# Down projection, attention output and denominators moved onto two 64-row tiles of the array

## The chip, the cores and the metric

The kernel runs on one core of a Trainium2 chip. The metric is device time in microseconds (us) of one execution. Its profile is one execution taken by the hardware profiler.

## What is computed

One block of a transformer on 2048 tokens of width 576: a layer norm, then linear attention with 32 heads of 18 and a gated feed-forward layer (FFN) of width 4608, both on the normed input, both added to the input. Cut to what matters:

```python
xn = layernorm(x)
q, k, v = split_heads(xn @ wqkv)                  # 32 heads of 18
phi = lambda t: where(t > 0, t + 1, exp(t)) + 1e-6
pq, pk = phi(q), phi(k)
kv = einsum("bhsd,bhse->bhde", pk, v)
z = einsum("bhsd->bhd", pk)
o = einsum("bhqd,bhde->bhqe", pq, kv) / (einsum("bhqd,bhd->bhq", pq, z)[..., None] + 1e-6)
out = x + o @ wo + (gelu(xn @ w_gate) * (xn @ w_up)) @ w_down
```

## The kernel before, in words

The order of instructions on each engine is the order of the program; a framework adds the semaphores. Work goes in three parts.

**Attention, to about 65.7 us.** Steps listed with due times (`STEPS`, lines 486 to 503, sorted at 535) norm the 16 tiles of 128 tokens, transpose them, compute the keys' phi and the sums over tokens. Queries are kept transposed in `pqT`: five chunks of heads (7, 7, 7, 7 and 4 heads: four times 126 rows, then 72) by 2048 tokens. `zrep` and `kvT` hold, per chunk, the sums of keys repeated per head and the key-value products, masked to the heads' diagonal blocks.

**FFN, gate and up** (`gu_pair`, line 615). The tokens go in four groups of 512 (`sc`), the 4608 hidden columns in blocks of 256. The contraction over 576 is four and a half tiles of 128 rows, so it is done on two tiles of the array of 64 rows each: a `_Unit` (line 302) has two outputs in two PSUM banks. In its first turn (`p1`) the lower rows feed output 0 while the upper rows feed output 1; in its second turn (`p2`) they change over. The units are built so that the two row tiles take turns on a bank; between the turns stands a relay: an empty instruction on another engine waits for the last matmul of the first turn, and the second turn waits for it (lines 322 and 323, 328 and 329). For gate and up the relay is on SyncE in the very first block and on GpSimd in all later ones (line 630). Between the two turns of a unit stands the other unit's first turn. ScalarE applies GELU (line 647), VectorE multiplies by the up half and writes `hT` (line 648). The eight PSUM banks go round in a ring, `banks`.

**FFN, down** (`down_tile`, line 664). For each of the four groups, the four tiles of 128 tokens are done in two halves of 288 output columns: 36 matmuls over `hT` and `wd_sb` (line 677), then five more that add the attention's output (line 682): `pqT`, by then divided by the denominators, times `m_sb`. Each is a full matmul of 128 rows (126 or 72 for the attention). VectorE adds the input and writes the result (line 685), SyncE stores it.

Two things lie inside the down stages. In the first one, `m_stage` (line 654) computes `m_sb`, the product of `kvT` and the output weights, chunk by chunk before steps 0, 6, 12, 18 and 24 of the first half, copied out by ScalarE (line 662). In the first three, the denominators of the next 512 tokens are made: one chunk per half tile, starting with the second, before its step 0 (`dn`, line 704): a matmul of `zrep` by `pqT` (`den_mm`, line 448), an evacuation by VectorE (line 445), four reciprocals by VectorE and the scaling of `pqT` by GpSimd (`den_norm`, lines 469 to 478). The denominators of tokens 0 to 511, and of the fifth chunk of tokens 512 to 1023, were made during the first gate and up blocks as units on two row tiles (`den_pair`, line 454).

**Start.** The x tiles 4 to 15 and the query weights are loaded by SyncE after VectorE has written two elements of x tile 4 (the step at time 4.0, lines 532 to 534), so that step sets when those loads begin.

Of the kernel before, what the change touches and what calls it, by code (L numbers as in the profile page):

```python
# [9 lines left out]
ALU = mybir.AluOpType  # L10
BF16 = mybir.dt.bfloat16
# [16 lines left out]
HALF = D // 2  # L28
KT = 5
HCH = [7, 7, 7, 7, 4]  # L30
HOFF = [0, 7, 14, 21, 28]
NCH = len(HCH)
CR = 7 * DH
# [23 lines left out]
def kernel(  # L57
# [11 lines left out]
    nc = tc.nc  # L69
# [12 lines left out]
    fwork = ctx.enter_context(tc.tile_pool(name="fwork", bufs=3))  # L82
# [9 lines left out]
    def load_x(n0, cnt):  # L92
        nc.sync.dma_start(x_sb[:, n0:n0 + cnt, :], x_view[:, n0:n0 + cnt, :])
# [47 lines left out]
    zrep = persist.tile([P, NCH, CR], BF16, name="zrep")  # L141
    kvT = persist.tile([P, NCH, CR], BF16, name="kvT")

    nc.vector.memset(pqT[HP:P, NCH - 1, 0:2 * SC], 0.0)
    nc.vector.memset(zrep[HP:P, NCH - 1, :], 0.0)

    def load_wo():
        nc.sync.dma_start(wo2[:CR, 0:4, :], A_wo[0:4 * CR, :].rearrange("(c p) j -> p c j", p=CR))
# [153 lines left out]
    class _Unit:  # L302
# [12 lines left out]
                start=start, stop=stop, skip_group_check=True,  # L315
            )

        def p1(self):
            for kt in self.first:
                self.mm(0, LO, kt, kt == self.first[0], False)  # L320
                last = self.mm(1, HI, kt, kt == self.first[0], False)
            self.turn = self.relay.nop()
            tc.add_manual_dep(self.turn.ins, last.ins.name, SYNC, reason="the row tiles take turns on a bank")

        def p2(self):
            for kt in self.then:
                m = self.mm(1, LO, kt, False, kt == self.then[-1])
# [114 lines left out]
    def den_evac(sc, c, ps):  # L442
        rows = DH * HCH[c]
        d = dwork.tile([P, SC], F32, name="den_sb", tag="den_sb", bufs=6)
        nc.vector.tensor_scalar_add(out=d[:rows, :], in0=ps, scalar1=EPS_ATT)
        den_sb[sc, c] = d

    def den_mm(sc, c, bank):
        rows = DH * HCH[c]
        ps = ps_all[:rows, bank, :]  # L450
        nc.tensor.matmul(ps, lhsT=zrep[:rows, c, :rows], rhs=pqT[:rows, c, sc * SC:(sc + 1) * SC], start=True, stop=True)  # L451
        den_evac(sc, c, ps)

    def den_pair(items, outs):

        rows = DH * HCH[items[0][1]]

        def part(r):

            return slice(r.start, min(r.stop, P if rows <= P - HP + 8 else rows))  # L460

        return _Unit(
            outs,
            lambda i, r, kt: zrep[part(r), items[i][1], :rows],
            lambda i, r, kt: pqT[part(r), items[i][1], items[i][0] * SC:(items[i][0] + 1) * SC],
            nc.sync, first=(0,), then=(0,),
        )

    def den_norm(sc, c, q, pieces):
        w = SC // pieces  # L470
        rows = DH * HCH[c]
        d = den_sb[sc, c][:rows, q * w:(q + 1) * w]
        cols = slice(sc * SC + q * w, sc * SC + (q + 1) * w)
        for h in range(0, w, P):
            nc.vector.reciprocal(out=d[:, h:h + P], in_=d[:, h:h + P])  # L475

        def scale():
            nc.gpsimd.tensor_tensor(out=pqT[:rows, c, cols], in0=pqT[:rows, c, cols], in1=d, op=ALU.mult)  # L478
        return scale
# [135 lines left out]
    def gu_pair(sc, k):  # L615
        cs = slice(sc * SC, (sc + 1) * SC)
        blk = sc * (NF // GUB) + k
        wg, wu, wr = gu_blocks.pop(blk)
        units = []
        for i in range(GUB):  # L620
            b = [banks.next(), banks.next()]
            fcol = slice(i * P, (i + 1) * P)

            def lhs(a, rows, kt, fcol=fcol):
                if kt == 4:
                    return wr[rows, fcol]
# [12 lines left out]
        den = None  # L639
        if sc == 0 and 0 <= k - DEN_FROM < len(DEN_PAIRS):  # L640
            items = DEN_PAIRS[k - DEN_FROM]
            den = den_pair(items, [ps_all[:DH * HCH[c], banks.next(), :] for _, c in items])
            den.p1()
        for i, (b, u) in enumerate(units):
            u.p2()
            gl = fwork.tile([P, SC], F32, name="gl")
            nc.scalar.activation(out=gl[:], in_=ps_all[:, b[0], :], func=ACT.Gelu_apprx_tanh)  # L647
            nc.vector.tensor_tensor(out=hT[:, GUB * k + i, :], in0=ps_all[:, b[1], :], in1=gl[:], op=ALU.mult)  # L648
# [5 lines left out]
    def m_stage(c, acc_bank):  # L654
        rows = DH * HCH[c]
        for hf in range(2):
            b = (acc_bank + 2 + (2 * c + hf) % 6) % 8
            hs = slice(hf * HALF, (hf + 1) * HALF)
            nc.tensor.matmul(  # L659
                ps_all[:rows, b, :HALF], lhsT=kvT[:rows, c, :rows], rhs=wo2[:rows, c, hs], start=True, stop=True,  # L660
            )
            nc.scalar.copy(out=m_sb[:rows, c, hs], in_=ps_all[:rows, b, :HALF])

    def down_tile(sc, j, hooks):
        n = sc * TPC + j
        ts_ = slice(n * P, (n + 1) * P)
        res = fwork.tile([P, D], BF16, name="res")
        last = n == NS - 1
        for hf in range(2):
            hs = slice(hf * HALF, (hf + 1) * HALF)  # L670
            todo = hooks.pop(0) if hooks else {}
            acc_bank = banks.next()
            acc = ps_all[:, acc_bank, :HALF]
            for f in range(NF):
                if f in todo:
                    todo[f](acc_bank)
                nc.tensor.matmul(  # L677
                    acc, lhsT=hT[:, f, j * P:(j + 1) * P], rhs=wd_sb[:, f, hs], start=(f == 0), stop=False,
                )
            for c in range(NCH):  # L680
                rows = DH * HCH[c]
                nc.tensor.matmul(  # L682
                    acc, lhsT=pqT[:rows, c, ts_], rhs=m_sb[:rows, c, hs], start=False, stop=(c == NCH - 1),
                )
            nc.vector.tensor_tensor(out=res[:, hs], in0=acc, in1=x_sb[:, n, hs], op=ALU.add)  # L685
            if last:
                nc.sync.dma_start(out_view[:, n, hs], res[:, hs])
        if not last:
            nc.sync.dma_start(out_view[:, n, :], res[:])

    for sc in range(NSC):
        for k in range(NF // GUB):
            gu_pair(sc, k)
            if scales:
                scales.pop(0)()
            if den_jobs and k > DEN_FROM:
                scales.append(den_norm(*den_jobs.pop(0)))
        while wd_loaded[0] < NF:
            load_wd_slice()

        hooks = [{6 * c_: (lambda b, c_=c_: m_stage(c_, b)) for c_ in range(NCH)} if sc == 0 else {}]
        if sc + 1 < NSC:
            for c_ in range(NCH):
                def dn(b, c=c_, nsc=sc + 1):
                    if (nsc, c) not in den_sb:
                        den_mm(nsc, c, (b + 2) % 8)
                    den_norm(nsc, c, 0, 1)()
                hooks.append({0: dn})
        for j in range(TPC):
            down_tile(sc, j, hooks)  # L710


# [28 lines left out]
```

## Time and profile before

| what | us |
|---|---|
| median of 3 runs (523.57 to 524.0) | 523.75 |
| the profiled execution | 523.47 |
| its span, first to last instruction | 521.7 |
| attention, 0 to 65.7 | 65.7 |
| gate and up, four groups | 77.2, 70.05, 70.0, 70.05 |
| down, four groups, the last one with the end of the kernel | 42.5, 41.45, 41.4, 43.35 |

How to read the lines that follow in the prediction: a row of forty digits is the span cut in forty slices, each digit the busy share in tenths; PEclk is the clock granted to TensorE. "L313 PE MATMUL ps_all<-xnT,wg 64\*128 64x512 bf16 x1152 | 272.6, 376 | 0.0" is a group: line, engine, operation, output and inputs, rows by columns of weights, shape, count, then busy time in us and mean ns of one, then the engine's idle time ahead of them. Matmuls are pipelined, so the length of one (286 ns for 288 columns) is longer than the distance from one to the next. A timeline line has the start in us, the length, the engine, the line and the instruction; in brackets, how long the engine had been idle and what ended that.

### The profile page before, as it was taken

What the parts mean: (1) busy time and instruction counts of PE and PEld (TensorE: products, weight loads), DVE (VectorE), ACT (ScalarE), POOL (GpSimd) and SP (SyncE); (2) the same over time, 40 slices, a digit from 0 to 9 for tenths busy, and PEclk for the clock granted to TensorE, in tenths of its full rate; (3) what the DMA queues carried; (4) which work ended last, traced back from release to release, by engine and by line L of the source; (5) the groups of instructions that cost most, each with busy time, mean ns of one, the idle gap of its engine ahead of it and who ended that gap; (6) DMA issues with size and microseconds to landing.
All of it is one profiled execution on the core that took longest, in us unless ns stands there. A gap on an engine that the chain in (4) does not pass through costs nothing.

```text
span 521.7 us, 10641 instructions
## 1 busy us (share of the span) xinstructions
PE 516.1 (99%) x4498; PEld 313.5 (60%) x4498; DVE 250.9 (48%) x436; ACT 143.1 (27%) x293; POOL 35.2 (7%) x55
## 2 busy tenths in 40 slices
PE   7999999999999999999999999999999999999997
PEld 6777755555587754444577744444777544445775
DVE  7996565876358323433388133333584233433101
ACT  6898442332320013323200032232000123322000
POOL 2021000211001100000012000000011000000000
PEclk9999999999999999999999999999999999999999
DMA  8334609899500045555300155555100355440000
GB/s 279 62 64 118 154 25 264 254 269 266 157 12 13 13 124 155 144 156 160 93 13 13 41 166 145 155 156 155 29 23 13 103 161 158 140 134 2 13 11 24
DMA packets 106282, 57.89 MB, mean 111 GB/s; under 512 B 13370, under 2 KB 105722, under 8 KB 106234
## 3 DMA queue, kind: packets, MB, share of 16 engines
q1 hardware_dynamic: 105626, 56.55, 38.8%
q8 instruction: 35, 0.57, 0.5%
q10 hardware_dynamic: 608, 0.66, 0.4%
q14 instruction: 13, 0.11, 0.1%
HBM read 52.86 MB, written 2.36 MB: 106 GB/s over the span
## 4 chain that ended last, share of the span: by engine, by line
PE 97%; DMA 1%; ACT 1%; DVE 0%; issue 0%
PE ps_all L313 55%; PE ps_all L677 27%; PE ps_all L289 4%; PE ps_all L682 4%; PE ps_all L245 3%; PE ps_all L342 3%; DMA wqkv_sb<-in_A_wqkv_dram 1%; PE ps_all L451 1%; PE ps_all L433 0%; PE ps_all L659 0%; ACT xnT L234 0%; ACT L114 0%; ACT phi_e L265 0%; ACT phi_e L269 0%; DVE hT L273 0%; DVE res L685 0%
## 5 line engine op out<-in xcount | busy, mean ns | idle before, releaser
L313 PE MATMUL ps_all<-xnT,wg 64*128 64x512 bf16 x1152 | 272.6, 376 | 0.0
L313 PE MATMUL ps_all<-xnT,wu 64*128 64x512 bf16 x1152 | 271.8, 376 | 0.0
L648 DVE TENSOR_TENSOR hT<-ps_all,gl 128x512 bf16<-128x512 f32 x144 | 99.5, 691 | 161.9 <-ACT gl L647 161.2
L647 ACT ACTIVATE gl<-ps_all 128x512 f32<-128x512 f32 x144 | 86.1, 598 | 314.3 <-PE ps_all L313 297.4
L313 PEld LDWEIGHTS <-wu 64*128 64x128 bf16 x1152 | 108.3, 94 | 66.3
L313 PEld LDWEIGHTS <-wg 64*128 64x128 bf16 x1152 | 108.3, 94 | 66.1
L677 PE MATMUL ps_all<-wd_sb,hT 128*128 128x288 bf16 x1152 | 147.0, 286 | 0.0
L677 PEld LDWEIGHTS <-hT 128*128 128x128 bf16 x1152 | 112.3, 98 | 30.6 <-issue 1.3
L475 DVE RECIPROCAL den_sb<-den_sb 126x128 f32<-126x128 f32 (+1 forms) x80 | 68.3, 911 | 0.5
L685 DVE TENSOR_TENSOR res<-ps_all,x_sb 128x288 bf16<-128x288 f32 x32 | 14.7, 458 | 88.0 <-PE ps_all L682 88.0
L313 PE MATMUL ps_all<-xnT,wr 64*128 64x512 bf16 x288 | 55.1, 376 | 0.0
L478 POOL TENSOR_TENSOR pqT<-pqT,den_sb 126x512 bf16<-126x512 bf16 (+3 forms) x25 | 24.2, 966 | 317.3 <-DVE den_sb L475 279.4
L682 PE MATMUL ps_all<-m_sb,pqT 126*128 126x288 bf16 (+1 forms) x160 | 24.9, 285 | 0.0
L313 PEld LDWEIGHTS <-wr 64*128 64x128 bf16 x288 | 14.4, 94 | 16.9 <-issue 0.7
L245 PE MATMUL ps_all<-wqkv_sb,xnT 128*128 128x288 bf16 x160 | 22.5, 286 | 0.9 <-DMA wqkv_sb<-in_A_wqkv_dram 0.8
L289 PE MATMUL ps_all<-hT,xn 128*128 128x288 bf16 (+4 forms) x176 | 22.4, 275 | 0.0
L289 PEld LDWEIGHTS <-xn 128*128 128x128 bf16 (+1 forms) x176 | 17.5, 102 | 4.1
L245 PEld LDWEIGHTS <-xnT 128*128 128x128 bf16 x160 | 15.4, 98 | 6.9 <-issue 1.4
L682 PEld LDWEIGHTS <-pqT 126*128 126x128 bf16 (+1 forms) x160 | 15.5, 97 | 4.1
L342 PE MATMUL ps_all<-xnT,wqkv_sb 128*126 128x512 bf16 (+1 forms) x70 | 17.4, 378 | 0.0
L273 DVE SCALAR_TENSOR_TENSOR hT<-ps_all,phi_e 128x288 bf16<-128x288 f32 x32 | 13.2, 450 | 4.6 <-ACT phi_e L269 4.0
L265 ACT ACTIVATE phi_e<-ps_all 128x288 f32<-128x288 f32 x32 | 12.9, 410 | 3.6 <-PE ps_all L245 2.1
(68 smaller groups left out, 173.8 us busy)
## 6 DMA issues: line engine op xcount, KB each, us to landing
wg<-in_B_w_gate_dram SPq DMA_DIRECT2D x72, 256.0 KB, 2.9
wu<-in_B_w_up_dram SPq DMA_DIRECT2D x72, 256.0 KB, 3.5
wd_sb<-in_B_w_down_dram SPq DMA_DIRECT2D x12, 432.0 KB, 4.6
wr<-in_B_w_gate_dram SPq DMA_DIRECT2D x72, 32.0 KB, 2.7
wr<-in_B_w_up_dram SPq DMA_DIRECT2D x72, 32.0 KB, 3.1
out_dram<-res SPq DMA_DIRECT2D x15, 144.0 KB, 1.8
x_sb<-in_A_x_dram SPq DMA_DIRECT2D x3, 576.0 KB, 7.1
wqkv_sb<-in_A_wqkv_dram SPq DMA_DIRECT2D x2, 576.0 KB, 4.7
```

Source lines behind the costliest of these rows:

```text
L245: nc.tensor.matmul(ps_all[:, k_bank(n, hf), :HALF], lhsT=xnT[:, kt, n * P:(n + 1) * P], rhs=wqkv_sb[:, kt, D + hf * HALF:D + (hf + 1) * HALF],
L273: nc.vector.scalar_tensor_tensor(out=out_, in0=ps, scalar=0.0, in1=e, op0=ALU.max, op1=ALU.add)
L289: nc.tensor.matmul(ps_all[:m, b, col:col + w], lhsT=xn[:, n, j0:j0 + m], rhs=pk[:, n, d0:d0 + w], start=(n == 0 and col == 0), stop=(n == ...
L313: return nc.tensor.matmul(self.outs[i], lhsT=self.lhs(i, rows, kt), rhs=self.rhs(i, rows, kt), start=start, stop=stop, skip_group_check=True,)
L342: nc.tensor.matmul(ps, lhsT=wqkv_sb[:, kt, q0:q0 + rows], rhs=xnT[:, kt, sc * SC:(sc + 1) * SC], start=(kt == 0), stop=(kt == KT - 1),)
L475: nc.vector.reciprocal(out=d[:, h:h + P], in_=d[:, h:h + P])
L478: nc.gpsimd.tensor_tensor(out=pqT[:rows, c, cols], in0=pqT[:rows, c, cols], in1=d, op=ALU.mult)
L647: nc.scalar.activation(out=gl[:], in_=ps_all[:, b[0], :], func=ACT.Gelu_apprx_tanh)
L648: nc.vector.tensor_tensor(out=hT[:, GUB * k + i, :], in0=ps_all[:, b[1], :], in1=gl[:], op=ALU.mult)
L677: nc.tensor.matmul(acc, lhsT=hT[:, f, j * P:(j + 1) * P], rhs=wd_sb[:, f, hs], start=(f == 0), stop=False,)
L682: nc.tensor.matmul(acc, lhsT=pqT[:rows, c, ts_], rhs=m_sb[:rows, c, hs], start=False, stop=(c == NCH - 1),)
L685: nc.vector.tensor_tensor(out=res[:, hs], in0=acc, in1=x_sb[:, n, hs], op=ALU.add)
```

## The change

* The four down stages do their tiles as units on two row tiles (`down_unit`), 41 steps per turn: 36 over `hT`, five for the attention. Output 0 is the first 288 columns, output 1 the rest. The first turn of tile j + 1 stands between the two turns of tile j. The relay is on ScalarE. The very last tile stays on full matmuls (`down_last`).
* A down stage takes its banks as four pairs `p[0]` to `p[3]`. Tile j uses `p[j % 3]`.
* The product for `m_sb` is made by units too (`m_unit`), before steps 9, 15, 21, 27 and 33 of the first tile's first turn, the second turn of each three steps later, in `p[3]` and `p[2]` by turns.
* All denominators of the next group are units (`den_pair`), in the second tile's first turn, first turns before steps 4, 16 and 28, second turns before steps 7, 19 and 31, all in `p[3]`. The evacuations of both chunks of a unit are followed at once by the reciprocals and the scaling of both. Group 1 (tokens 512 to 1023) has a third unit with the fifth chunk of groups 2 and 3. Where the fifth chunk was already there, its reciprocals and its scaling come after the last tile's output.
* The fifth chunk, 72 rows, is read to 128 rows, so `zrep`, `kvT`, `m_sb`, `wo2` and all of `pqT` are zeroed there at the start.
* The step that lets the x loads begin moves from time 4.0 to 5.0.

```diff
-    nc.vector.memset(pqT[HP:P, NCH - 1, 0:2 * SC], 0.0)
-    nc.vector.memset(zrep[HP:P, NCH - 1, :], 0.0)
+    nc.vector.memset(pqT[HP:P, NCH - 1, :], 0.0)
+    for t in (zrep, kvT, m_sb, wo2):
+        nc.vector.memset(t[HP:P, NCH - 1, :], 0.0)
...
-        def p1(self):
+        def p1(self, hooks=()):
             for kt in self.first:
+                if kt in hooks:
+                    hooks[kt]()
...
-    todo += [(4.0, lambda n: nc.vector.memset(x_sb[0:1, n, 0:2], 0.0), 4)]
-    todo += [(4.01, lambda n: load_x(n, 4), n) for n in (4,)]
-    todo += [(4.02, lambda n: load_w(0), 0)] + [(4.03, lambda n: load_x(n, 4), n) for n in (8, 12)]
+    todo += [(5.0, lambda n: nc.vector.memset(x_sb[0:1, n, 0:2], 0.0), 4)]
+    todo += [(5.01, lambda n: load_x(n, 4), 4), (5.02, lambda n: load_w(0), 0)]
+    todo += [(5.03, lambda n: load_x(n, 4), n) for n in (8, 12)]
...
+    def m_unit(c, b):
+        rows = DH * HCH[c]
+        return _Unit(
+            [ps_all[:rows, b + i, :HALF] for i in range(2)],
+            lambda i, r, kt: kvT[part(r, c), c, :rows],
+            lambda i, r, kt: wo2[part(r, c), c, i * HALF:(i + 1) * HALF],
+            nc.scalar, first=(0,), then=(0,),
+        )
...
+    def down_unit(n, b):
+        sc, j = divmod(n, TPC)
+        ts_ = slice(n * P, (n + 1) * P)
+
+        def lhs(i, r, kt):
+            return hT[r, kt, j * P:(j + 1) * P] if kt < NF else pqT[part(r, kt - NF), kt - NF, ts_]
+
+        def rhs(i, r, kt):
+            hs = slice(i * HALF, (i + 1) * HALF)
+            return wd_sb[r, kt, hs] if kt < NF else m_sb[part(r, kt - NF), kt - NF, hs]
+
+        steps = range(NF + NCH)
+        return _Unit([ps_all[:, b + i, :HALF] for i in range(2)], lhs, rhs, nc.scalar, steps, steps)
...
+    def run_turns(step, units, first, gap, done):
+
+        hooks = {}
+        for i, u in enumerate(units):
+            hooks[first + step * i] = u.p1
+
+            def end(u=u, i=i):
+                u.p2()
+                done(i, u)
+            hooks[first + step * i + gap] = end
+        return hooks
+
+    def down(sc):
+
+        p = [banks.tiles[(banks.i + 2 * k) % 8] for k in range(4)]
+        n0 = sc * TPC
+        last = sc == NSC - 1
+        u = [down_unit(n0 + j, p[j % 3]) for j in range(TPC - last)]
+        hooks = [{}, {}]
+        if sc == 0:
+            ms = [m_unit(c, p[3 - c % 2]) for c in range(NCH)]
+            hooks[0] = run_turns(6, ms, 9, 3, m_copy)
         if not last:
-            nc.sync.dma_start(out_view[:, n, :], res[:])
+            items = [[(sc + 1, 0), (sc + 1, 1)], [(sc + 1, 2), (sc + 1, 3)]]
+            if (sc + 1, NCH - 1) not in den_sb:
+                items.append([(sc + 1, NCH - 1), (sc + 2, NCH - 1)])
+            dens = [den_pair(it, [ps_all[:DH * HCH[c], p[3] + i, :] for i, (_, c) in enumerate(it)], nc.scalar) for it in items]
+
+            def den_out(k, unit):
+                for (dsc, c), ps in zip(items[k], unit.outs):
+                    den_evac(dsc, c, ps)
+                for dsc, c in items[k]:
+                    if dsc == sc + 1:
+                        den_norm(dsc, c, 0, 1)()
+            hooks[1] = run_turns(12, dens, 4, 3, den_out)
+        u[0].p1(hooks[0])
+        for j in range(1, len(u)):
+            u[j].p1(hooks[1] if j == 1 else ())
+            u[j - 1].p2()
+            down_out(n0 + j - 1, u[j - 1].outs)
+        u[-1].p2()
+        down_out(n0 + len(u) - 1, u[-1].outs)
+        if last:
+            down_last(NS - 1, p[0])
+        elif (sc + 1, NCH - 1) in den_sb and len(items) == 2:
+            den_norm(sc + 1, NCH - 1, 0, 1)()
+        banks.i += 2
```

More of the change, by code (lines that the diff above doesn't have):

```diff
@@ L323, in p1, with p2 @@
             tc.add_manual_dep(self.turn.ins, last.ins.name, SYNC, reason="the row tiles take turns on a bank")
-        def p2(self):
+        def p2(self, hooks=()):
             for kt in self.then:
+                if kt in hooks:
+                    hooks[kt]()
                 m = self.mm(1, LO, kt, False, kt == self.then[-1])
@@ L446, in den_evac, with part, den_pair @@
         den_sb[sc, c] = d
[L448 to L454, printed above, removed]
+    def part(r, c):
+        return slice(r.start, P if c == NCH - 1 else CR) if r is HI else r
+    def den_pair(items, outs, relay):
         rows = DH * HCH[items[0][1]]
-        def part(r):
-            return slice(r.start, min(r.stop, P if rows <= P - HP + 8 else rows))
         return _Unit(
             outs,
-            lambda i, r, kt: zrep[part(r), items[i][1], :rows],
-            lambda i, r, kt: pqT[part(r), items[i][1], items[i][0] * SC:(items[i][0] + 1) * SC],
-            nc.sync, first=(0,), then=(0,),
+            lambda i, r, kt: zrep[part(r, items[i][1]), items[i][1], :rows],
+            lambda i, r, kt: pqT[part(r, items[i][1]), items[i][1], items[i][0] * SC:(items[i][0] + 1) * SC],
+            relay, first=(0,), then=(0,),
         )
@@ L641, in gu_pair @@
             items = DEN_PAIRS[k - DEN_FROM]
-            den = den_pair(items, [ps_all[:DH * HCH[c], banks.next(), :] for _, c in items])
+            den = den_pair(items, [ps_all[:DH * HCH[c], banks.next(), :] for _, c in items], nc.sync)
             den.p1()
@@ L652, in gu_pair, with m_copy @@
                 den_evac(dsc, c, ps)
-    def m_stage(c, acc_bank):
+    def m_unit(c, b):
[6 more added lines that the diff above has]
+        )
+    def m_copy(c, u):
         rows = DH * HCH[c]
         for hf in range(2):
-            b = (acc_bank + 2 + (2 * c + hf) % 6) % 8
-            hs = slice(hf * HALF, (hf + 1) * HALF)
[L659 to L662, printed above, removed]
@@ L664, in down_tile @@
-    def down_tile(sc, j, hooks):
-        n = sc * TPC + j
+            nc.scalar.copy(out=m_sb[:rows, c, hf * HALF:(hf + 1) * HALF], in_=u.outs[hf])
+    def down_unit(n, b):
[8 more added lines that the diff above has]
+        return _Unit([ps_all[:, b + i, :HALF] for i in range(2)], lhs, rhs, nc.scalar, steps, steps)
@@ L666, in down_tile, with down_out, down_last @@
+    def down_out(n, outs):
+        res = fwork.tile([P, D], BF16, name="res")
+        for hf in range(2):
+            hs = slice(hf * HALF, (hf + 1) * HALF)
+            nc.vector.tensor_tensor(out=res[:, hs], in0=outs[hf], in1=x_sb[:, n, hs], op=ALU.add)
+        nc.sync.dma_start(out_view[:, n, :], res[:])
+    def down_last(n, b):
         ts_ = slice(n * P, (n + 1) * P)
         res = fwork.tile([P, D], BF16, name="res")
-        last = n == NS - 1
         for hf in range(2):
             hs = slice(hf * HALF, (hf + 1) * HALF)
-            todo = hooks.pop(0) if hooks else {}
-            acc_bank = banks.next()
-            acc = ps_all[:, acc_bank, :HALF]
+            acc = ps_all[:, b + hf, :HALF]
@@ L674, in down_tile @@
             for f in range(NF):
-                if f in todo:
-                    todo[f](acc_bank)
                 nc.tensor.matmul(
-                    acc, lhsT=hT[:, f, j * P:(j + 1) * P], rhs=wd_sb[:, f, hs], start=(f == 0), stop=False,
-                )
+                    acc, lhsT=hT[:, f, (n % TPC) * P:(n % TPC + 1) * P], rhs=wd_sb[:, f, hs], start=(f == 0), stop=False)
             for c in range(NCH):
@@ L682, in down_tile @@
                 nc.tensor.matmul(
-                    acc, lhsT=pqT[:rows, c, ts_], rhs=m_sb[:rows, c, hs], start=False, stop=(c == NCH - 1),
-                )
+                    acc, lhsT=pqT[:rows, c, ts_], rhs=m_sb[:rows, c, hs], start=False, stop=(c == NCH - 1))
             nc.vector.tensor_tensor(out=res[:, hs], in0=acc, in1=x_sb[:, n, hs], op=ALU.add)
-            if last:
-                nc.sync.dma_start(out_view[:, n, hs], res[:, hs])
-        if not last:
-            nc.sync.dma_start(out_view[:, n, :], res[:])
+            nc.sync.dma_start(out_view[:, n, hs], res[:, hs])
@@ L699 @@
             load_wd_slice()
[L701 to L710, printed above, removed]
+        down(sc)
 _INS = ['A_x', 'A_wqkv', 'A_wo', 'B_x', 'B_w_gate', 'B_w_up', 'B_w_down']
```

## The prediction, made before the changed kernel ran

> **What bounds the kernel now.** I read the chain that ended last first, then the costliest groups, then the timeline around one border between gate/up and down, and last what VectorE and GpSimd do in a down stage. From the page:
>
> ```profile
> PE   7999999999999999999999999999999999999997
> ...
> PEclk9999999999999999999999999999999999999999
> ...
> PE 97%; DMA 1%; ACT 1%; DVE 0%; issue 0%
> ...
> L313 PE MATMUL ps_all<-xnT,wg 64*128 64x512 bf16 x1152 | 272.6, 376 | 0.0
> ...
> L677 PE MATMUL ps_all<-wd_sb,hT 128*128 128x288 bf16 x1152 | 147.0, 286 | 0.0
> ```
>
> TensorE is the path: 97% of the chain, no idle before its big groups, full clock. So a change gains only what it takes out of TensorE's own time, and every wait that it puts in front of a matmul counts in full. The border at 185 us, in the timeline of TensorE (start, length, line):
>
> ```profile
> 184.70 0.78 PE L682 MATMUL ps_all<-m_sb,pqT 126*128 126x288 bf16 x5
> 185.41 0.39 PE L313 MATMUL ps_all<-xnT,wr 64*128 64x512 bf16 x2
> 185.64 0.38 PE L313 MATMUL ps_all<-xnT,wg 64*128 64x512 bf16 x1
> ```
>
> Cadences are read from starts. In the down stage 36 matmuls of 288 columns follow at 0.1225 us; five from 184.70 should hand over at 185.31, and the 64-row mode begins at 185.41: 0.10 us lost. A pair of 64-row matmuls of 512 columns takes 0.2159 us (648 matmuls from 185.411 to 255.139). VectorE in the down stage of the first 512 tokens, then ScalarE and GpSimd:
>
> ```profile
> 143.66 0.69 DVE L648 TENSOR_TENSOR hT<-ps_all,gl 128x512 bf16<-128x512 f32 x1 [0.17 <-ACT gl L647]
> 149.44 0.46 DVE L685 TENSOR_TENSOR res<-ps_all,x_sb 128x288 bf16<-128x288 f32 x1 [5.09 <-PE ps_all L682]
> 149.82 0.68 DVE L445 TENSOR_SCALAR den_sb<-ps_all 126x512 f32<-126x512 f32 x1
> 150.53 3.39 DVE L475 RECIPROCAL den_sb<-den_sb 126x128 f32<-126x128 f32 x4
> ...
> 170.81 3.37 DVE L475 RECIPROCAL den_sb<-den_sb 72x128 f32<-72x128 f32 x4
> ```
> ```profile
> 145.27 0.70 ACT L662 CAST m_sb<-ps_all 126x288 bf16<-126x288 f32 x2 [0.28 <-PE ps_all L659]
> ```
> ```profile
> 174.26 1.16 POOL L478 TENSOR_TENSOR pqT<-pqT,den_sb 72x512 bf16<-72x512 bf16 x1 [3.29 <-DVE den_sb L475]
> ```
>
> To see: before, one denominator chunk (evacuation 0.68, four reciprocals 3.39) fits into each half tile of 5.25 us, so its queue never grows; and the last scaling on GpSimd stands at 174.26, 11 us ahead of the next gate/up stage.
>
> [...] 0.10 us above, 0.09 on the way in (142.621 to 142.926 less a pair's 0.216). [...] The trace shows only the warm-up: 128-column warm-up matmuls at 0.107 us until 4.6 us, then 0.056. [...] on ScalarE the semaphore event of the next GELU, whose condition was old, stands at 87.134, just after the GELU that had waited 2.86 us starts at 87.128, and so all along.
>
> **Part by part.**
> 1. *Mode changes.* Before: four entries to down and three exits. A whole down stage (255.447 to 296.646, 41.20 us) is 0.06 above its cadence, so an entry costs about 0.15 and an exit 0.11. After: one entry remains, before the last tile, which stays on 128 rows. 3 x 0.15 + 3 x 0.11 = **-0.8**.
> 2. *Down on two row tiles.* 15 tiles x 82 pairs = 1,230 pairs in place of as many full matmuls. The trace has no 288-column pair. Streaming is the same; four instructions per 0.1225 us, and loads of 94 ns on each tile, must fit. In the gate/up stage both tiles' loads start together, and L433 shows a 72-column load and matmul 0.030 after one another, so they fit. Per pair I take +0.15 ns, between -2 (512 columns cost no more per pair than one full matmul) and +5: **+0.2** (-2.5 to +6). M and denominators are likewise streamed equally: 10 matmuls become 10 pair slots, 14 become 14.
> 3. *Relays.* The turn is an event on ScalarE, which holds nothing waiting then. After a pair's last matmul (0.286 or 0.376) the event follows 0.04 later, lasts 0.017; three down pairs (0.37) plus the pair itself cover it: **+0.1**. Between tiles a whole half (5 us) covers it.
> 4. *M in the first down stage.* Unit 0 uses the last gate/up unit's banks at its step 9, 142.84 + 9 x 0.1225 = 143.94; the product at 143.66 frees them at 144.35: 0.45. The last M unit runs just before step 36; its two copies end 1.03 after it starts (144.94 to 145.97 before), step 40 wants them after 5 x 0.1225 = 0.61: 0.45 with the signal. **+0.9**. Before, M was twelve steps earlier.
> 5. *Denominators.* All of a stage now come in the second tile's first half, at steps 4, 16, 28, all in one bank pair, with evacuations and reciprocals on VectorE in that order, two chunks per unit: 2 x 0.68 + 8 x 0.85 = 8.2 us of VectorE per 12 steps of 1.47. The order of the changed kernel's instructions shows units 1 and 2 waiting for VectorE. From the start t of unit 0's second turn: evacuations end t + 0.42 + 1.32 = t + 1.74; unit 1 is due at 0.216 + 9 x 0.1225 = t + 1.32. So +0.47 in three stages: **+1.4**. Only tokens 512 to 1023 have a third unit. It needs unit 1's evacuations, which stand behind unit 0's eight reciprocals: 1.74 + 6.8 + 1.36 = t + 9.9. It is due at 1.79 + 0.58 + 0.22 + 1.10 = t + 3.7. **+6.2**. The queue then still holds 12 reciprocals and ends 28 us into the stage; the first tile's output waits there, but its banks are wanted only at 33, so that hides.
> 6. *Clock.* That stall is 5.6 us of silence. [...] Price: as in the warm-up, 30 matmuls at 0.107 in place of 0.056, **+1.5** [...].
> 7. *Entry to the next gate/up stage.* In stages 0 and 2 the last chunk's reciprocals are issued after the last tile's output, and GpSimd's scaling after them; gate/up's relays are on GpSimd, behind that scaling. From TensorE's last down slot G: outputs G + 0.2 to 1.08, reciprocals to 4.45, scaling dispatched (0.08 later, as 174.18 to 174.26) G + 4.53, matmul G + 4.65. Due: after two first turns of five pairs, G + 2.16. 2 x 2.5 = **+5.0**. Behind the wait: both first units' second turns, hence GELU and product. Nothing if events pass.
> 8. *Start.* More zeroing on VectorE: by L119 (864 words, 0.778) and L144 (512, 0.485), 512 + 63 + 288 + 288 more words cost 1.1; 0.5 of idle before the first statistics hides part. The x loads go 1.4 us later; tiles 4 to 7 landed near 8 us and are used at 10.35, so that hides, as do the queries' weights behind them (used at 13.3). The K weights, waited for 0.79, may come sooner. **+0.3** (-0.8 to +0.6).
>
> Sum: -0.8 + 0.2 + 0.1 + 0.9 + 1.4 + 6.2 + 1.5 + 5.0 + 0.3 = +14.8, on the profiled execution's 523.47 (span 521.7): 538.3. The median of the runs is 523.75, 0.3 above, so I say **538.5**.
>
> **Rivals.**
> *Events pass waiting instructions on GpSimd* (15%): item 7 goes; 533.5. [...] against: ScalarE's events, 6 ns behind each started GELU. ScalarE's own relays would not change.
> *Pairs of 288 columns don't keep up* (7%): loads of 94 ns on both tiles or four instructions per slot set the pace. 5 ns a pair is 6.2 us: 544.5. Against it: the 0.030 spacing in L433.
> *It ends faster* (4%): denominators and scaling turn out to wait for nothing, because the order of issue leaves VectorE's queue shorter than I count, and what remains is the mode change, 0.8, and at most 2.5 of pair overhead: 523.47 - 3.3 + 1.0 = 521.2. This decides only if items 5 and 7 together stay under about 1 us; items 4 and 1 already cancel. Against it: 20 reciprocals of 0.85 must pass between steps 7 and 28, which is 2.6 us of TensorE.
> *It doesn't change the mode count*: the instruction order shows 64-row loads through M, denominators and 15 tiles, so no.
>
> **How the numbers follow.** Forecast 74%, the rivals 15, 7 and 4. Within the forecast the clock may stay up (536.8) and the pair overhead runs either way. Low end 532: GpSimd's rival without the clock's drop. High end 543: half of the pair overhead's bound and a longer cold spell. About 2 in 10 lie outside. This kernel's measurement tells 0.2% (1 us) from no change; faster by more 3%, within 2%, slower 95%.
>
> **What would show it.** In the profile after: one TensorE wait of some 6 us for VectorE's evacuation in the second down stage, with granted clock under 1 after it; two of 2.5 us at the starts of gate/up for tokens 512 and 1536, none at 1024; pairs of 288 columns at 0.1225; no 0.1 us gaps at the borders. Wrong: no wait in the second stage, or pairs above 0.125.

## The result and the profile after

The changed kernel takes 541.06 us (539.02 to 541.64, 4 runs) where the kernel before takes 523.66 (523.46 to 524.0) beside it: a ratio of 1.0325, 95% interval 1.0297 to 1.0352. Forecast was 538.5 in a range of 532 to 543. The profiled execution took 540.99, its span is 539.3 and its mean granted clock 0.987; before, the span was 521.7 and the clock 1.000.

From the page of the changed kernel, the rows that were shown of the kernel before (the lines moved by one: L314 is the matmul of every unit):

```profile
PE   8999999999999989999969999999999899999997
...
PEclk9999999999999989999979999999999899999999
...
PE 81%; issue 9%; DVE 7%; DMA 1%; ACT 1%; POOL 0%; DVEq 0%; POOLq 0%
...
L314 PE MATMUL ps_all<-xnT,wu 64*128 64x512 bf16 x1152 | 271.2, 379 | 4.2 <-POOLq L325 4.2
...
L314 PE MATMUL ps_all<-wd_sb,hT 64*128 64x288 bf16 x2160 | 146.3, 284 | 0.0
```

Before, only the first and the last slice of the PE row stood below nine tenths, and no slice of the clock's row did. Now three more slices of the PE row do, and the clock falls in the same three. The chain gives 7% to VectorE, which stood at 0. The waits view of TensorE (engine, the line that waits, the releaser: us in total, times, longest) names them:

```profile
PE ps_all L314 <- DVE den_sb L450: 5.4, 3, 5.0
PE ps_all L314 <- POOLq L325: 4.2, 2, 2.1
...
PE ps_all L314 <- DVE hT L647: 0.2, 1, 0.2
```

Two words that come back below: a slot is the time from one matmul (or pair on the two row tiles) to the next, 0.1225 us for 288 columns, and a matmul hands over when its slot ends. In tables, "after" is the changed kernel.

**The long wait.** TensorE in the second down stage, the timeline of the changed kernel:

```profile
269.48 1.32 PE L314 MATMUL ps_all<-wd_sb,hT 64*128 64x288 bf16 x18
275.82 1.17 PE L314 MATMUL ps_all<-pqT,zrep 64*72 64x512 bf16 x2 [5.02 <-DVE den_sb L450]
```

VectorE at that place:

```profile
267.40 1.29 DVE L450 TENSOR_SCALAR den_sb<-ps_all 126x512 f32<-126x512 f32 x2 [5.07 <-PE ps_all L314]
268.60 6.62 DVE L474 RECIPROCAL den_sb<-den_sb 126x128 f32<-126x128 f32 x8
275.14 1.22 DVE L450 TENSOR_SCALAR den_sb<-ps_all 126x512 f32<-126x512 f32 x2
276.28 6.62 DVE L474 RECIPROCAL den_sb<-den_sb 126x128 f32<-126x128 f32 x8
```

The third unit wants the banks of the second. Their evacuation, at 275.14, stands behind the eight reciprocals of the first, which hold VectorE from 268.60 to 275.14. The first of the two evacuations at 275.14 lasts some 0.6 us, and at 275.82 the unit's first matmul starts; the other row tile's, which needs the second evacuation, starts at 276.41.

**The two short waits.** The start of gate and up for tokens 512 to 1023 (187 to 191.4), TensorE, VectorE and GpSimd:

```profile
188.85 0.38 PE L314 MATMUL ps_all<-xnT,wu 64*128 64x512 bf16 x1
191.33 0.60 PE L314 MATMUL ps_all<-xnT,wu 64*128 64x512 bf16 x1 [2.11 <-POOLq L325]
```
```profile
187.10 0.82 DVE L687 TENSOR_TENSOR res<-ps_all,x_sb 128x288 bf16<-128x288 f32 x2 [4.21 <-PE ps_all L314]
187.84 3.37 DVE L474 RECIPROCAL den_sb<-den_sb 72x128 f32<-72x128 f32 x4
```
```profile
191.30 1.15 POOL L477 TENSOR_TENSOR pqT<-pqT,den_sb 72x512 bf16<-72x512 bf16 x1 [22.65 <-DVE den_sb L474]
```

The first turns had been done at 189.23. The reciprocals end at 191.22. Only then do the two instructions go that GpSimd holds in this order: the scaling, recorded from 191.30, and the relay behind it, an event that the trace has at 191.26. TensorE goes on at 191.33. The same stands at 423.86 (tokens 1536 to 2047); at 1024 there is none.

**The clock.** The windows view of the same core (stretch, its length, busy us and count of PE, PE's loads, VectorE, ScalarE and GpSimd, granted clock, DMA share, GB/s), ahead of the first short wait's end and in the 3.4 us after it:

```profile
186.78:191.37 4.59, 2.48 (x27) 1.73 (x24) 4.11 (x6) 0.00 (x0) 0.07 (x1) 1.00 0.40 106
191.37:194.79 3.42, 3.42 (x18) 1.21 (x20) 0.69 (x1) 0.60 (x1) 1.08 (x1) 0.50 0.25 74
194.79:198.00 3.21, 3.21 (x34) 1.43 (x32) 0.69 (x1) 0.60 (x1) 0.00 (x0) 1.00 0.43 112
```

and around the long one:

```profile
273.29:275.90 2.61, 0.08 (x1) 0.08 (x1) 2.61 (x5) 0.00 (x0) 0.60 (x1) 0.50 0.00 0
275.90:280.12 4.22, 4.21 (x31) 3.29 (x32) 4.22 (x6) 0.00 (x0) 0.88 (x2) 0.50 0.00 0
280.12:284.00 3.88, 3.88 (x67) 3.88 (x64) 3.88 (x7) 0.00 (x0) 1.86 (x2) 1.00 0.02 4
```

The clock is halved for a stretch after each of the three waits: 191.37 to 194.79, 273.29 to 280.12 and 426.89 to 430.31. At half clock TensorE did half the work: 18 matmuls in 3.42 us, then 34 in 3.21.

**Where the time is, stage by stage.** From the first matmul of a stage to that of the next, us:

| stage | before | after | difference |
|---|---|---|---|
| up to the first gate/up, with it | 142.93 | 143.10 | +0.17 |
| down, tokens 0 to 511 | 42.49 | 43.72 | +1.23 |
| gate/up, 512 | 70.04 | 73.98 | +3.95 |
| down, 512 | 41.42 | 49.37 | +7.95 |
| gate/up, 1024 | 70.04 | 69.93 | -0.11 |
| down, 1024 | 41.42 | 41.73 | +0.31 |
| gate/up, 1536 | 70.04 | 73.98 | +3.94 |
| down, 1536, to the end | 43.38 | 43.47 | +0.08 |

The differences sum to 17.5, and the spans (521.75 and 539.27 before rounding) differ by as much.

### The profile page after: what moved, and what is told of

It is laid out like the page before. It is cut to its first block, busy times and chain, and to the rows that moved or that the text cites. A ratio compares the mean times of both kernels' runs of the same rounds, so it can differ in the third digit from the quotient of the medians.

```text
span 539.3 us, 13167 instructions
## 1 busy us (share of the span) xinstructions
PE 523.9 (97%) x5752; PEld 345.9 (64%) x5752; DVE 248.4 (46%) x439; ACT 143.1 (27%) x293; POOL 35.1 (7%) x55
## 3 DMA queue, kind: packets, MB, share of 16 engines
HBM read 52.86 MB, written 2.36 MB: 102 GB/s over the span
## 4 chain that ended last, share of the span: by engine, by line
PE 81%; issue 9%; DVE 7%; DMA 1%; ACT 1%; POOL 0%; DVEq 0%; POOLq 0%
PE ps_all L314 69%; DVE den_sb L474 6%; PE ps_all L290 4%; PE ps_all L246 3%; PE ps_all L347 3%; PE ps_all L698 2%; DVE den_sb L450 1%; DMA wqkv_sb<-in_A_wqkv_dram 1%; POOL pqT L477 0%; PE ps_all L438 0%; PE ps_all L702 0%; ACT xnT L235 0%; ACT L114 0%; ACT phi_e L266 0%; DVE hT L647 0%
## 5 line engine op out<-in xcount | busy, mean ns | idle before, releaser
L314 PE MATMUL ps_all<-xnT,wg 64*128 64x512 bf16 x1152 | 276.1, 379 | 0.0
L314 PE MATMUL ps_all<-xnT,wu 64*128 64x512 bf16 x1152 | 271.2, 379 | 4.2 <-POOLq L325 4.2
L314 PEld LDWEIGHTS <-wu 64*128 64x128 bf16 x1152 | 107.3, 95 | 71.3 <-POOLq L325 5.2
L314 PEld LDWEIGHTS <-wg 64*128 64x128 bf16 x1152 | 108.9, 95 | 64.3 <-issue 1.3
L314 PE MATMUL ps_all<-wd_sb,hT 64*128 64x288 bf16 x2160 | 146.3, 284 | 0.0
L314 PEld LDWEIGHTS <-hT 64*128 64x128 bf16 x2160 | 130.5, 95 | 9.8 <-issue 2.5
L314 PE MATMUL ps_all<-xnT,wr 64*128 64x512 bf16 x288 | 63.8, 378 | 0.0
L687 DVE TENSOR_TENSOR res<-ps_all,x_sb 128x288 bf16<-128x288 f32 x30 | 12.1, 445 | 82.9 <-PE ps_all L314 82.9
L314 PEld LDWEIGHTS <-wr 64*128 64x128 bf16 x288 | 18.2, 95 | 16.0 <-issue 0.5
L314 PE MATMUL ps_all<-m_sb,pqT 64*128 64x288 bf16 (+1 forms) x300 | 27.2, 287 | 0.0
L314 PEld LDWEIGHTS <-pqT 64*128 64x128 bf16 (+1 forms) x300 | 20.0, 96 | 1.0 <-issue 0.2
L450 DVE TENSOR_SCALAR den_sb<-ps_all 126x512 f32<-126x512 f32 (+1 forms) x20 | 12.6, 669 | 17.4 <-PE ps_all L314 17.4
L290 PEld LDWEIGHTS <-xn 128*128 128x128 bf16 (+1 forms) x176 | 17.5, 101 | 4.1
L347 PE MATMUL ps_all<-xnT,wqkv_sb 128*126 128x512 bf16 (+1 forms) x70 | 17.4, 378 | 0.0
L314 PE MATMUL ps_all<-pqT,zrep 64*126 64x512 bf16 (+2 forms) x40 | 11.1, 405 | 5.6 <-DVE den_sb L450 5.4
```

Source lines behind the costliest of these rows:

```text
L290: nc.tensor.matmul(ps_all[:m, b, col:col + w], lhsT=xn[:, n, j0:j0 + m], rhs=pk[:, n, d0:d0 + w], start=(n == 0 and col == 0), stop=(n == ...
L314: return nc.tensor.matmul(self.outs[i], lhsT=self.lhs(i, rows, kt), rhs=self.rhs(i, rows, kt), start=start, stop=stop, skip_group_check=True,)
L347: nc.tensor.matmul(ps, lhsT=wqkv_sb[:, kt, q0:q0 + rows], rhs=xnT[:, kt, sc * SC:(sc + 1) * SC], start=(kt == 0), stop=(kt == KT - 1),)
L687: nc.vector.tensor_tensor(out=res[:, hs], in0=outs[hf], in1=x_sb[:, n, hs], op=ALU.add)
```

## The experiments

The theory is that of the prediction: the row tiles cost nothing, the array's modes gain a little, and the time is lost where TensorE waits behind work that the change put ahead of its releasers, the reciprocals on VectorE and the scaling on GpSimd. What the profile after adds is a larger part for the clock. The rivals are that the pairs themselves are slower, and that TensorE would wait at these places anyway.

**e1, relays off GpSimd.** In the first gate/up block of each group but the first (whose relay is on SyncE) ScalarE passes the turn.

```diff
-                      nc.sync if blk == 0 else nc.gpsimd)
+                      nc.sync if blk == 0 else nc.scalar if k == 0 else nc.gpsimd)
```

> Only the first gate/up block of each group has its two relays on ScalarE; reciprocals and scaling of the fifth chunk stay where they are. Theory (the relay stands behind GpSimd's scaling, which waits for VectorE): both waits of 2.27 us and both cold stretches of 3.41 us at half clock (1.7 us lost each) go, 541.1 - 7.9 = 533.2. Rival (VectorE's late queue itself holds the stage, the relay is only named): no gain, 541. Rival (the cold stretch comes from something else than the wait): 541.1 - 4.5 = 536.6.

Measured: 533.49 (532.92 to 533.96), ratio to before 1.0184 (1.0169 to 1.0200). No wait for GpSimd's queue is left, and both low-clock stretches in gate/up went with it. All that line 314 waits for in this kernel:

```profile
PE ps_all L314 <- DVE den_sb L450: 5.6, 4, 5.0
...
PE ps_all L314 <- DVE hT L647: 0.2, 1, 0.2
```

So 7.6 us hung on two relays that stood behind one scaling each. In the profiled execution the two gate/up stages lose 4.05 each, and the down stage with the long wait, still 5.0 long, grows by 1.1: its low-clock stretch lies later (271.15 to 277.98) and covers 6.4 us of work in place of 4.3. The scaling and the reciprocals are still there, at the same place; only what waits for them changed.

**e2, evacuations first.** The units in the down stage only evacuate; reciprocals and scaling come after the second tile's first half and after the outputs of the first two tiles.

```diff
-                for dsc, c in items[k]:
+
+            def norms(k):
+                for dsc, c in items[k] if not last and k < len(items) else ():
...
+            if j == 1 and not last:
+                norms(0)
             u[j - 1].p2()
             down_out(n0 + j - 1, u[j - 1].outs)
+            if j <= 2 and not last:
+                norms(j)
```

> The denominator units only evacuate during the second tile's first turn; their reciprocals and scalings come after it, after the first tile's output and after the second tile's output. The fifth chunk at the end of groups 0 and 2 stays. Theory (third unit of the second stage waits for evacuations that stand behind eight reciprocals): the wait of 5.56 us falls to about 0.3 as for the second unit, and the cold stretch behind it (4.3 us of work at half clock, 2.15 lost) goes: 541.1 - 7.4 = 533.7. Rival (VectorE simply has too much to do in that stage, so the wait moves to a later tile's bank): less than 3 us gained, 538 or more, with a new wait at the last tile's first turn.

Measured: 531.92 (530.77 to 532.03), ratio 1.0150 (1.0135 to 1.0165). VectorE's timeline in the second down stage of this kernel shows three evacuations ahead of all reciprocals:

```profile
267.09 1.29 DVE L450 TENSOR_SCALAR den_sb<-ps_all 126x512 f32<-126x512 f32 x2 [5.07 <-PE ps_all L314]
269.50 1.29 DVE L450 TENSOR_SCALAR den_sb<-ps_all 126x512 f32<-126x512 f32 x2 [1.12 <-PE ps_all L314]
271.91 1.28 DVE L450 TENSOR_SCALAR den_sb<-ps_all 72x512 f32<-72x512 f32 x2 [1.12 <-PE ps_all L314]
273.11 6.62 DVE L474 RECIPROCAL den_sb<-den_sb 126x128 f32<-126x128 f32 x8
```

and its waits of TensorE:

```profile
PE ps_all L314 <- POOLq L325: 4.2, 2, 2.1
...
PE ps_all L314 <- DVE den_sb L450: 0.6, 3, 0.2
```

The long wait is gone: 9.1 us less than the changed kernel, and 1.8 less than I had expected of it. The two waits for GpSimd stay as long as they were, but in the profiled execution only the first lowered the clock. That accounts for 1.7 of the 1.8: the second gate/up stage with a wait takes 72.29 us in place of 73.98. Such a wait thus has no fixed price. It shows in the changed kernel too: three of its four executions had a mean clock of 0.987 and took 541.0 to 541.6, the fourth had 0.990 and took 539.02.

**e3, both edits.**

> Both edits together. Theory (the two causes are independent and hold nearly all of the loss): 541.1 - 7.9 - 7.4 = 525.8, 2 us above the kernel before: M's waits 0.7, second denominator units 3 x 0.3, start 0.2, third unit 0.3, less the mode changes 0.8. Rival (they overlap, one wait takes the place of the other): 530 or more.

Measured: 525.94 (525.71 to 526.45), ratio 1.0044 (1.0027 to 1.0061). The clock stays up through the whole FFN. Waits of TensorE for VectorE, in this kernel:

```profile
PE ps_all L314 <- DVE den_sb L450: 0.8, 4, 0.2
PE ps_all L314 <- DVE hT L647: 0.2, 1, 0.2
```

Of the 17.4 us, 15.1 are explained by two orders of work. What is left is 2.3, and these small waits are the candidates, with those around M.

**e4, the waits stay but TensorE doesn't fall silent.** Into each of the three waits go thrown-away pairs of 64-row matmuls: 10, 23 and 10. The kernel leaves nothing out.

```diff
+        if k == 0 and sc in (1, 3):
+            fill(banks.tiles[banks.i % 8], 10)
...
+    def fill(b, pairs):
+        for _ in range(pairs):
+            for i, r in enumerate((LO, HI)):
+                nc.tensor.matmul(ps_all[:, b + i, :], lhsT=ident[r, :], rhs=xnT[r, 0, 0:SC],
+                                 start=True, stop=True, skip_group_check=True)
...
+            if len(dens) == 3:
+                third = hooks[1][28]
+                def filled():
+                    fill(p[2], 23)
+                    third()
+                hooks[1][28] = filled
```

> All waits stay; ahead of each of the three long ones TensorE gets matmuls into unused banks whose results nobody reads: 10 pairs of 512 columns (2.16 us) before the second turns of the first block of groups 1 and 3, 23 pairs (4.97 us) before the third denominator unit. They fill most of the silence and lengthen nothing if they end before the waits do. Theory (idle time lowers the clock afterwards, and that costs 1.7 + 1.7 + 2.15): full clock through the FFN and 541.1 - 5.6 = 535.5. Rival (the lower clock does not follow from the silence): clock lowered as before and 541 or a little more.

Measured: 536.00 (535.63 to 536.03), ratio 1.0231 (1.0216 to 1.0246). The clock of the profiled execution:

```profile
core 0: 534.3 us, clock 1.000
```

The page has no PEclk row; the trace holds no change of the clock. TensorE reaches the third unit and the two second turns as late as in the changed kernel (15.02 us into the down stage and 4.51 into gate and up, in both), and yet the kernel is 5.06 us faster than that. This is the clock's part alone: work that computes nothing buys 5 us. By stages it is 1.69 in each of the two gate/up stages and 1.67 in the second down stage.

**e5, the small waits too.** On top of e2: the fifth chunk's reciprocals and scaling also come after the second tile's output, 10 us ahead of the next gate/up; the denominator units alternate between two bank pairs; the units for M begin at step 5 in pairs that are free earlier.

```diff
-            ms = [m_unit(c, p[3 - c % 2]) for c in range(NCH)]
-            hooks[0] = run_turns(6, ms, 9, 3, m_copy)
+            ms = [m_unit(c, p[2 + c % 2]) for c in range(NCH)]
+            hooks[0] = run_turns(6, ms, 5, 3, m_copy)
...
-            dens = [den_pair(it, [ps_all[:DH * HCH[c], p[3] + i, :] ...
+            dens = [den_pair(it, [ps_all[:DH * HCH[c], p[3 - k % 2] + i, :] ...
...
-                for dsc, c in items[k] if not last and k < len(items) else ():
+                for dsc, c in (items[k] if k < len(items) else [(sc + 1, NCH - 1)]):
...
-        elif (sc + 1, NCH - 1) in den_sb and len(items) == 2:
-            den_norm(sc + 1, NCH - 1, 0, 1)()
```

> The changed kernel with nothing left in VectorE's way. As in e2_evac the units in the down stage only evacuate, and the reciprocals and the scaling come after the outputs of the tiles; the fifth chunk's reciprocals and scaling now come after the second tile's output, 10 us ahead of the next gate/up stage. Besides, the denominator units alternate between two bank pairs, so that a unit no longer waits for the evacuations of the one before it, and the units for M begin at step 5 and lie in bank pairs that are free earlier. Theory (all that the change costs is bank waits and relays behind work on VectorE, ScalarE and GpSimd): from e3_both's 525.9 take the units' waits, 2.2, and those around M, 0.8: 522.9, so 0.15% below the kernel before, which is the mode changes. No TensorE wait above 0.2 us in the FFN, clock 1.0. Rival (row-tiled down pairs cost something themselves, by loads or by the turns): the waits go but the time stays at 524.5 or more.

Measured: 522.89 (522.82 to 523.6, 21 runs), before 523.65 (41 runs), ratio 0.9989 (0.9982 to 0.9995). From its page and, below it, all waits of its TensorE that the waits view lists, none of them in the FFN:

```profile
PE 97%; DMA 1%; ACT 1%; DVE 0%; issue 0%
...
L314 PE MATMUL ps_all<-wd_sb,hT 64*128 64x288 bf16 x2160 | 143.9, 282 | 0.0
```
```profile
PE ps_all L133 <- POOL ident masks.py:199: 1.4, 1, 1.4
PE ps_all L232 <- DVE xn L217: 0.6, 1, 0.6
PE ps_all L246 <- DMA wqkv_sb<-in_A_wqkv_dram: 0.3, 1, 0.3
```

It has all units, all row tiles and as many changes of mode as the changed kernel, and takes 18.2 us less. No run separates the three edits from each other. The rival of slow pairs is out: 2,160 of the 64-row matmuls run in a kernel that is not slower than the one with full ones. Against before, its gate/up stages are 0.11 shorter, four times (the change to the 128-row mode at their end, 0.11 in e7, is gone). Its down stages are 0.11 shorter at 0, 0.10 longer at 512 and 0.33 shorter at 1024. The last two hold a piece of work that changed place: one product of 0.216 (the fifth chunk of tokens 1536 to 2047, now made in one unit with that of tokens 1024 to 1535) moved from the third stage to the second. Without it all three are 0.11 shorter (the change back to the 64-row mode, 0.10 in e7, is gone). The last stage is 0.15 longer; it has the one change to the 128-row mode that remains, ahead of the last tile.

**e6, the start.** e5 with the added zeroing on GpSimd in place of VectorE.

```diff
-    nc.vector.memset(pqT[HP:P, NCH - 1, :], 0.0)
-    for t in (zrep, kvT, m_sb, wo2):
-        nc.vector.memset(t[HP:P, NCH - 1, :], 0.0)
+    nc.vector.memset(pqT[HP:P, NCH - 1, 0:2 * SC], 0.0)
+    nc.vector.memset(zrep[HP:P, NCH - 1, :], 0.0)
...
+    for t in (kvT, m_sb, wo2):
+        nc.gpsimd.memset(t[HP:P, NCH - 1, :], 0.0)
...
+    nc.gpsimd.memset(pqT[HP:P, NCH - 1, 2 * SC:], 0.0)
```

> e5_hide with the added zeroing moved from VectorE to GpSimd. Theory (item 8 of the prediction, the start costs 0.3): 0.3 below e5_hide. Rival (the later x loads hide it, as the spans of e1 to e3 suggest): the same as e5_hide within 0.1.

Measured: 523.09 (522.12 to 523.6, 21 runs), ratio 0.9987 (0.9981 to 0.9994): the same as e5. The zeroing costs nothing that 21 runs can tell. The first gate/up matmul stands at 71.86 in e5, 71.88 in e6 and the changed kernel, 71.59 before; but also at 71.57 to 71.60 in e1 to e3 and at 72.06 in e4, which have the changed kernel's start unaltered. So it shifts by up to 0.5 between executions of one and the same start.

**e7, the price of a mode by itself.** The kernel before, with a thrown-away pair of 64-row matmuls ahead of 24 half tiles.

```diff
+            if sc > 0:
+                for i, r in enumerate((LO, HI)):
+                    nc.tensor.matmul(ps_all[:, (acc_bank + 4) % 8 // 2 * 2 + i, :HALF], lhsT=ident[r, :],
+                                     rhs=xnT[r, 0, 0:HALF], start=True, stop=True, skip_group_check=True)
```

> The kernel before, with one thrown-away pair of 64-row matmuls of 288 columns in front of each of the 24 half tiles in the down stages of groups 1 to 3, into a bank pair that nothing else uses then. 21 of them stand between two halves and add one exit from the 64-row mode and one entry to the 128-row mode each; the three at the start of a stage stand in 64-row mode already. Theory (item 1, entry 0.15 and exit 0.11): 24 x 0.1225 of streaming, 2.9, and 21 x 0.26, 5.5: 523.7 + 8.4 = 532.1. Rival (a change of mode costs nothing, the 0.1 seen at the borders is something else there): 526.6.

Measured: 533.40 (533.11 to 533.97), ratio 1.0189 (1.0173 to 1.0204): 9.75 more than before where 8.4 was expected. TensorE's timeline in the last down stage of this kernel:

```profile
506.48 0.78 PE L686 MATMUL ps_all<-m_sb,pqT 126*128 126x288 bf16 x5
507.19 0.29 PE L676 MATMUL ps_all<-xnT,ident 64*128 64x288 bf16 x2
507.42 0.79 PE L681 MATMUL ps_all<-wd_sb,hT 128*128 128x288 bf16 x5
```

Five full matmuls from 506.48 would hand over at 507.09; the pair starts at 507.19: 0.10. The pair would hand over at 507.31; the next full one starts at 507.42: 0.11. In this stage, which makes no denominators, the distance from half to half is 5.36 us in place of 5.03, 0.33 more, of which 0.12 is the pair's streaming: **0.21 for both changes**. That is under the 0.26 of item 1. So 21 half tiles are 7.0. At the start of each stage the inserted pair wants a bank that VectorE still reads (0.4 of wait), and these three starts cost 0.83 each, 2.5. The remaining 0.3 is in the two stages that make denominators, which grew by 0.17 each more than the last; why, no run separates. So the total was above what was expected although the change of mode itself is cheaper.

## Why the prediction was right, and its mis-sized term

The prediction was right in direction, in the places of the three waits, in their lengths to within a sixth, and in putting GpSimd's rival and that of slow pairs second. Its total is 2.6 below the measurement: one term was 3.5 too small, and the others together 0.9 too large, so that the total is nearer than that one term is luck. Three kernels' stages take the loss apart. e4 has the waits of the changed kernel at full clock, e5 has neither waits nor low clock, so "after" less e4 is the clock's part and e4 less e5 the waits':

| stage | after | e4 | e5 |
|---|---|---|---|
| down, 0 | 43.72 | 43.72 | 42.37 |
| gate/up, 512 | 73.98 | 72.30 | 69.93 |
| down, 512 | 49.37 | 47.69 | 41.52 |
| down, 1024 | 41.73 | 41.61 | 41.09 |
| gate/up, 1536 | 73.98 | 72.29 | 69.93 |

Item by item:

| item | said | measured | from |
|---|---|---|---|
| 1 modes | -0.8 | -0.6 | stages of e5 against before: 4 x -0.107, 3 x -0.11, +0.15 |
| 2 pairs | +0.2 | 0.0 | a down stage of e5, some 330 pairs: 0.11 shorter, and the exit alone is 0.10 at the border before |
| 3 relays | +0.1 | 0.0 | the same row |
| 4 M | +0.9 | +0.8 | down at 0: after less e5 1.35, less 0.52 for the second unit |
| 5 second units | +1.4 | +1.6 | down at 1024: e4 less e5 0.52, three times |
| 5 third unit | +6.2 | +5.6 | down at 512: e4 less e5 6.17, less 0.52 for the second unit |
| 6 clock | +1.5 | +5.0 | after less e4: 1.69, 1.67 and 1.69 |
| 7 entries | +5.0 | +4.7 | gate/up at 512 and 1536: e4 less e5 2.37 and 2.36 |
| 8 start | +0.3 | +0.3 or 0 | varies by execution |
| sum | 14.8 | 17.4 | of 17.5 between the spans |

In the changed kernel the down stage at 1024 is 0.12 longer than in e4: one row tile had run that much further ahead of the other when it began, and no longer when it ended.

**The mis-sized term is item 6, the clock: 5.0 in place of 1.5.** e4 measures it by itself, with all waits kept: 5.06 between the medians. Two steps of its working were off. First, it put a clock drop only behind the 5.6 us stall and none behind the two waits at gate/up. That was an estimate of mine that no trace had shown: before, the clock stands at 1.00 from 4.60 us on, and its only fall, at 523.42, lies behind the last matmul. After, it fell behind both of the shorter ones: the first is silent only from 189.23 to 191.33, 2.1 us, and the clock fell at 191.37. Second, I priced a drop as a warm-up of 30 short matmuls, 1.5; the low stretches behind these two are 3.413 us long, and at half clock that is 1.7. The long wait, with 6.827 us at half clock, cost the same 1.67, because TensorE had work in only 4.3 us of them, and in the first 0.6 us of that one row tile still waited for its evacuation.

Item 7 stood for the two waits and was right: the relays on GpSimd did not pass the scaling that waited ahead of them. In the first of the two places, the relay behind the scaling fired at 191.26, 0.04 after the end of the reciprocals that the scaling waited for and well before the scaling's own end (192.45), and e1 takes both waits away by moving nothing but the relay. ScalarE had shown the same order in the kernel before (an event at 87.134, behind a GELU that had waited and started at 87.128). Each wait was 0.13 cheaper than forecast: the matmul came 4.51 after the last down slot's hand-over (186.82 to 191.33) in place of 4.65. The row tile that was due first, at 2.16 as said, lost 2.36, the other, due 0.09 later, 2.27.

Item 5's long wait was right in cause, shown by e2, and 0.6 us too long. From the first unit's second turn (266.90) the third was due at 3.74, as said, and came at 8.92 in place of 9.9: the reciprocals run at 0.83 in a row (8 in 6.62), not at 0.85, and the unit's first matmul needs only the first of two evacuations; the other row tile's starts 0.6 later (276.41), so the stage loses more than that first matmul. Its shorter part, 0.47 per stage (its own 1.74 less 1.32 is 0.42), measured 0.52: in the down stage at 1024 the row tile that waits was due at 387.75 and starts at 388.26, the other loses 0.36.

Item 1's cost of an entry, 0.15, was the excess of a whole stage over its cadence and included more than the change of mode; both changes are 0.10 to 0.11. In the changed kernel the border shows none of it: ten attention matmuls from 186.21, at 0.1225 a pair, hand over at 186.82, and that is where gate/up starts.

```profile
186.21 0.86 PE L314 MATMUL ps_all<-m_sb,pqT 64*128 64x288 bf16 x10
186.82 0.47 PE L314 MATMUL ps_all<-xnT,wr 64*128 64x512 bf16 x2
```

So the change does what it says. It removes 0.6 us of mode changes and pays 18 for it in the order of the work around it. e5 keeps the removal and none of the pay, at 0.1% below the kernel before; that is all that the modes are worth here.

## What to carry to other kernels

An empty instruction that passes a turn belongs on an engine that holds nothing waiting at that moment; behind a step that waits for a third engine, it makes the array wait for that engine too (two such relays were worth 7.6 us, e1). When a bank is to be used again soon, issue its evacuation before the arithmetic on what was evacuated earlier, and count how long that arithmetic holds the queue against the distance to the next use (here eight reciprocals, 6.62 us, stood ahead of the evacuation; e2, which turns that order round, is 9.1 us faster, 1.7 of it by a clock that stayed up elsewhere). And add the clock to the price of a wait of the array before it is set against a gain of tenths: here a wait of 2.1 us cost between nothing (once in e2) and 1.7 us more than its length, and one of 5.0 us cost 1.7 more, in e1 2.8 (1.7 and the 1.1 by which that stage grew).

## What the runs showed of the hardware that I had not expected

The clock fell behind waits shorter than the 3.41 us of its low stretch. That length is also the step in which the clock changed: in the changed kernel the six changes that follow the one at 7.05, up to 430.31, come 54, 55, 78, 80, 123 and 124 times 3.413 us after it; in the kernel before, 4.60 and 523.42 are 152 times as much apart. With windows of this length laid from the edges of the low records, and the silence counted from the end of one matmul to the start of the next:

| kernel, window | silent in it | clock after it |
|---|---|---|
| after, 187.96 to 191.37 | 2.11 | falls |
| after, 269.88 to 273.29 | 2.49 | falls |
| after, 273.29 to 276.71 | 2.53 | stays low |
| after, 276.71 to 280.12 | 0 | rises |
| after, 423.48 to 426.89 | 2.11 | falls |
| e2, 188.69 to 192.10 | 2.10 | falls |
| e2, 413.97 to 417.38 | 0.52 | stays high |
| e2, 417.38 to 420.79 | 1.59 | stays high |
| e1, 264.32 to 267.74 | 1.35 | stays high |
| e1, 267.74 to 271.15 | 3.41 | falls |
| e1, 271.15 to 274.56 | 0.43 | stays low |
| e7, 527.23 to 530.64, behind the last matmul | 1.94 | falls |
| after, 3.64 to 7.05, at the start | 0.58 | rises |

On these thirteen windows, the clock falls after 1.94 us of silence or more, and doesn't after 1.59. For the way up silence alone doesn't decide: low, it stayed so after a window with 0.43, yet at the start of the changed kernel it rose after one with 0.58 (matmuls of 128 columns follow at 0.107 us until 7.06 and at 0.056 from there). In the window with 0.43, one row tile stood still 0.6 us longer than the other (its first matmul is at 272.17, the other's at 271.58). The same wait of 2.1 us, in e2, fell once into one window and once across two, and only the first time did it cost the clock. No run varied the length of a wait on purpose, so whether a limit lies between 1.59 and 1.94, and whether it is silence or work that counts, stays open.
